# Loading a convolution filter by DMA in 64-byte runs, already in the layout of its first matmul, in place of transposing it on the matrix engine

## The chip, the cores and the metric

The kernel runs on one core of a Trainium2 chip. The metric is device time in microseconds (us), the median of several runs; lower is better. A ratio is computed as the mean time of one kernel's runs over that of the other's of the same rounds, so it is not quite the ratio of the medians quoted beside it.

## The reference, cut to what matters

The program is the forward and backward pass of two branches in parallel on a 2048 x 1024 bf16 input: a gated MLP (the larger part of the work) and a long convolution (H3) whose filter `ssm_k` is as long as the sequence. The convolution is written with FFTs:

```python
kv = k_shift * v                                  # (1, 2048, 1024)
kv_f = rfft2(pad(kv))                             # over time
kf_f = rfft2(pad(ssm_k))                          # ssm_k is (1024 channels, 2048 times)
y = irfft2(kv_f * kf_f)[:2048] + kv * ssm_D
out = x + xn * y + mlp(xn)                        # and the gradients of it all
```

One thing matters here: `ssm_k` lies in memory by channel, its times side by side, while `kv` and the gradients lie by time. The transform runs over time, so on the matrix engine time must lie on the partitions.

## The kernel before: the parts that the change and the argument touch

The convolution branch goes through 8 groups of 128 channels. Its transform is split in two steps of small matmuls with tables of sines. Its instructions are spread over slots between the MLP's matmuls, one slot per 8 of these, so that the matrix engine (PE) always has MLP work while ACT (ScalarE) and DVE (VectorE) serve the branch. The filter of a group is loaded with channels on the partitions, transposed on the matrix engine in sixteen pieces, and run through the first step:

```python
    def loads_1(self, gi):
        hn = self.ld.tile([P, 16, P], BF16, name="hn")
        self.load(hn[:].rearrange("p r c -> p (r c)"), self.ssm_k[cg, :])        # 128 rows of 4096 bytes
        ...                                                                      # gt, sD

    def h_tile(self, st):
        hT = self.ttile("hT")
        hv = st["hn"][:].rearrange("p r c -> p (r c)").rearrange("p (q r) -> p r q", r=16)
        pst = self.ps.tile([P, 16, P], BF16, name="pst", tag="aps")
        for r in range(16):
            self.pri.now()
            self.pri.pin(self.nc.tensor.transpose(pst[:, r, :], hv[:, r, :], self.identA[:]))
        self.act(hT[:, 0:16, :], pst[:])
        return hT

    def fwd1_filter(self, st, hT):                     # RH: the sine table R, with every other row zero
        B = st["Bh"] = self.big.tile([P, 64, NB1, 2], BF16, name="B", tag="big")
        for r0 in range(0, NB1, 8):                    # four steps, each in its own slot
            ps = self.ps.tile([P, 1024], F32, name="ps0", tag="aps")       # two PSUM buffers
            for jj in range(2):
                r = r0 % 16 + 4 * jj
                self.mm(ps[:, 512 * jj:512 * jj + 512], self.RH[:, r0 // 16]..., hT[:, r:r + 4, :]...)
            self.act(B[:, :, r0:r0 + 8, :], ps[:]...)                      # eviction on ACT
            yield
```

The gate gradient (`gt`, loaded by time) goes through the same first step in another form: 64 times on the lower and 64 on the upper half of the partitions, one matmul with 64 rows for each half.

```python
                for u in range(2):
                    rows = slice(64 * u, 64 * u + 64)
                    self.mm(ps[:, u]..., self.R[rows]..., src[rows, j:j + 4, :]...)
```

The names in the lines shown below: hn is the filter, gt the gate gradient, xt the normalised input by time, vt is v and kp is k; B is the result of a first step. The gate product is gt times xt, on DVE. wg, wu and wd are the gate, up and down weights of the MLP, and xnT its transposed input. An eviction is the copy of a result out of PSUM, the memory that the matmuls write to.

All loads of the branch, and nearly all others, are issued by the SyncE sequencer on one DMA queue (q1).

```python
    def steps(self):                                   # the start of the branch
        ...
        nx = self.loads_1(0); self.loads_2(nx)         # hn, gt, sD; kp, vt of group 0
        yield 10000 ... yield 13000 ... yield 9500     # waits, in ns of MLP work
        self.load_xn(nx)                               # xt of group 0
        hT = self.h_tile(nx)
        yield 2000
        ...                                            # the slots of group 0, 1, ... 7
```

## Time and profile before

| | before |
|---|---|
| median of the first 3 runs | 1920.11 us (1919.44 to 1923.64) |
| span of the profiled run | 1917.5 us |
| matrix engine (PE) busy | 98% |
| transposes / first-step matmuls of the filter | 128 / 64 |
| DMA packets, of them under 512 bytes | 628,002, 458,360 |

The lines that carry this are shown in the prediction. How to read them: a line of the timeline gives the start and the duration in us, then engine, source line, operation and tiles; `x8` is a run of eight instructions; brackets give the idle time before it and what ended it.

### The profile page before, as it was taken

The page shows a single profiled execution, that of the slowest core. Times are in us where ns is not written, and L with a number is a line of the kernel's source. Part 1 is how long each engine was busy: PE and PEld are TensorE (multiplying, and loading weights), DVE is VectorE, ACT ScalarE, POOL GpSimd, SP SyncE. Part 2 cuts the span into 40 slices and gives each one's busy share as a digit, 9 for nine tenths or more (in the row PEclk, how much of TensorE's full clock was granted, in tenths as well). Part 3 has the DMA queues.
Part 4 walks back from the last instruction along what each step waited for, and adds up shares of the span by engine and source line. Part 5 has one row for each costly group of instructions (what it writes and reads, how often), then busy time and mean ns, then how long its engine had stood idle before and what let it go on. Part 6 is the DMA issues. An engine that isn't in the chain of part 4 may idle for free.

```text
span 1917.5 us, 36080 instructions
## 1 busy us (share of the span) xinstructions
PE 1887.5 (98%) x15343; PEld 885.7 (46%) x15575; DVE 911.3 (48%) x1365; ACT 635.4 (33%) x868; POOL 15.8 (1%) x38
## 2 busy tenths in 40 slices
PE   8999999999999999999999999999999999999999
PEld 4444444444444444444444444444444544444444
DVE  6777767767767754544444354310212222222222
ACT  5854364364364354354344344321000000000000
POOL 1100000000000000000000000000000000000000
PEclk9999999999999999999999999999999999999999
DMA  9975878974975972655662633375999964444453
GB/s 248 290 178 136 184 184 184 222 184 133 186 182 136 251 218 78 176 132 179 153 170 90 170 100 122 100 206 208 266 240 239 241 156 121 121 121 121 121 121 72
DMA packets 628002, 323.16 MB, mean 169 GB/s; under 512 B 458360, under 2 KB 597376, under 8 KB 627840
## 3 DMA queue, kind: packets, MB, share of 16 engines
q1 hardware_dynamic: 617344, 299.99, 63.5%
q10 hardware_dynamic: 9216, 16.65, 2.8%
q0 software_dynamic: 1280, 4.20, 0.7%
q8 instruction: 122, 2.00, 0.4%
q14 instruction: 40, 0.33, 0.1%
HBM read 143.79 MB, written 95.44 MB: 125 GB/s over the span
## 4 chain that ended last, share of the span: by engine, by line
PE 95%; DMA 2%; issue 1%; DVE 1%; SPq 0%; ACT 0%; DVEq 0%; ACTq 0%
PE ps_x L1294 20%; PE ps_w L1067 19%; PE ps_h L818 10%; PE ps_o L1225 10%; PE ps_u L818 10%; PE ps_g L818 9%; PE ps_d L1067 8%; PE ps L72 7%; PE ps_d L1080 1%; DMA wu<-in_B_W_up_dram 1%; DMA ugs<-ug_d 0%; DMA ln_x<-in_A_q_dram 0%; PE pst L308 0%; PE ps_w L1080 0%; DMA xt<-xn_d 0%
## 5 line engine op out<-in xcount | busy, mean ns | idle before, releaser
L1067 PE MATMUL ps_w<-ugs,xn_nat 128*128 128x512 bf16 x1673 | 376.7, 379 | 5.3 <-issue 3.7
L818 PEld LDWEIGHTS <-xnT 128*128 128x128 bf16 x1792 | 170.1, 98 | 211.6 <-issue 10.3
L1067 PEld LDWEIGHTS <-xn_nat 128*128 128x128 bf16 x1728 | 165.0, 98 | 199.4 <-issue 5.5
L818 PE MATMUL ps_g<-wg,xnT 128*128 128x512 bf16 x862 | 202.5, 379 | 5.5 <-DVE xnT L853 1.9
L818 PE MATMUL ps_u<-wu,xnT 128*128 128x512 bf16 x868 | 204.5, 379 | 3.2 <-issue 1.4
L1312 ACT ACTIVATE w<-xn,m 128x512 f32<-128x512 bf16 x32 | 24.3, 807 | 553.0 <-issue 317.2
L818 PE MATMUL ps_h<-wdT,goT 128*128 128x512 bf16 x868 | 202.0, 379 | 2.6 <-issue 1.6
L1294 PE MATMUL ps_x<-wuT,guT 128*128 128x512 bf16 x878 | 197.5, 379 | 1.0
L1294 PE MATMUL ps_x<-wgT,ggT 128*128 128x512 bf16 x878 | 197.3, 379 | 0.9
L1225 PE MATMUL ps_o<-wd,hT 128*128 128x512 bf16 (+1 forms) x879 | 186.7, 372 | 0.9
L1067 PE MATMUL ps_d<-g_nat,hs 128*128 128x512 bf16 x740 | 167.7, 379 | 3.1 <-issue 2.4
L1294 PEld LDWEIGHTS <-guT 128*128 128x128 bf16 x896 | 87.7, 98 | 105.7
L1294 PEld LDWEIGHTS <-ggT 128*128 128x128 bf16 x896 | 87.7, 98 | 105.5
L1225 PEld LDWEIGHTS <-hT 128*128 128x128 bf16 x896 | 87.7, 98 | 100.0
L818 PEld LDWEIGHTS <-goT 128*128 128x128 bf16 x896 | 85.4, 98 | 102.9 <-issue 3.4
L319 DVE STREAM_TRANSPOSE flp<-C 128x1024 f32<-128x1024 f32 x48 | 90.5, 1931 | 81.7 <-ACT C L76 81.7
L921 DVE SCALAR_TENSOR_TENSOR ru<-ru,ps_u 128x512 bf16<-128x512 bf16 x112 | 76.6, 684 | 110.3 <-issue 48.9
L984 ACT CAST gh<-ps_h 128x512 bf16<-128x512 f32 x112 | 65.4, 585 | 159.0 <-PE ps_h L818 150.6
L76 ACT CAST C<-ps 128x1024 bf16<-128x1024 f32 x96 | 92.5, 1015 | 75.6 <-PE ps L72 74.6
L1171 ACT CAST wi<-ps_w 128x512 bf16<-128x512 f32 x108 | 63.7, 590 | 157.1 <-PE ps_w L1067 144.8
L319 DVE STREAM_TRANSPOSE flp<-B 128x1024 f32<-128x1024 f32 x48 | 90.5, 1935 | 50.4 <-ACT B L76 50.4
L1067 PEld LDWEIGHTS <-hs 128*128 128x128 bf16 x768 | 72.7, 98 | 88.9 <-issue 4.2
(176 smaller groups left out, 1479.7 us busy)
## 6 DMA issues: line engine op xcount, KB each, us to landing
ug_d<-ru SPq DMA_DIRECT2D x112, 256.0 KB
ugs<-ug_d SPq DMA_DIRECT2D x112, 256.0 KB
wg<-in_B_W_gate_dram SPq DMA_DIRECT2D x56, 256.0 KB
wu<-in_B_W_up_dram SPq DMA_DIRECT2D x56, 256.0 KB
h_d<-ht SPq DMA_DIRECT2D x112, 128.0 KB
hs<-h_d SPq DMA_DIRECT2D x56, 256.0 KB
out_dram<-wi SPq DMA_DIRECT2D x56, 256.0 KB
gt<-in_grad_out_dram SPq DMA_DIRECT2D x32, 256.0 KB
```

Source lines behind the costliest of these rows:

```text
L72: self.pri.pin(self.nc.tensor.matmul(out, lhsT=lhsT, rhs=rhs, start=start, stop=stop))
L76: self.pri.pin(self.nc.scalar.copy(out=out, in_=in_))
L319: self.pri.pin(self.nc.vector.transpose(out=df[:, c0:c0 + 32, :], in_=sf[:, c0:c0 + 32, :]))
L818: self.pri.pin(self.nc.tensor.matmul(ps[:], lhsT=xT[:, kt * P:(kt + 1) * P], rhs=w(kt), start=(kt == 0), stop=(kt == self.DT - 1)), always ...
L921: self.pri.pin(nc.vector.scalar_tensor_tensor(out=ru[s][:, 1, :], in0=ru[s][:, 0, :], scalar=0.0, in1=ps[:], op0=ALU.is_gt, op1=ALU.mult))
L984: self.pri.pin(nc.scalar.copy(out=gh[:], in_=ps[:]))
L1067: self.pri.pin(self.nc.tensor.matmul(ps[:], lhsT=lhsT(st), rhs=rhs(st), start=(st == 0), stop=(st == self.ST - 1)))
L1080: self.pri.pin(self.nc.tensor.matmul(ps[i][:], lhsT=lhsT(i, st), rhs=rhs(i, st), start=(st == 0), stop=(st == self.ST - 1)))
L1171: self.pri.pin(nc.scalar.copy(out=wo[0][:, d, :], in_=ps[:]))
L1225: nc.tensor.matmul(ps, lhsT=hT[:, kt, :], rhs=self.wd[:, kt, oc], start=(kt == 0), stop=(kt == self.FT - 1))
L1294: nc.tensor.matmul(ps, lhsT=T[:, kt, :], rhs=W[:, kt, oc], start=(i == 0), stop=(i == n - 1))
L1312: nc.scalar.activation(out=w[:, oc], in_=xn[:, oc], func=ACT.Identity, scale=m[:, 7:8], bias=m[:, 6:7])
```

## The change

Its intent: let the DMA do the transposing. It reads each channel's row in runs of 32 times (64 bytes) and writes every run to the partition of its time block. Sixteen transposes, an eviction and a half-empty table per group go; the first step becomes that of the gate gradient. The core of the diff (cut: declarations, passing of `hT`):

```diff
-        self.load(hn[:].rearrange("p r c -> p (r c)"), self.ssm_k[cg, :])
+        for ch in range(2):
+            c0 = gi * P + 64 * ch
+            self.load(hn[64 * ch:64 * ch + 64], self.ssm_k[c0:c0 + 64, :].rearrange("c (q n) -> q c n", n=NB1))
...
-    def h_tile(self, st):
-        ... (16 transposes and a copy)
...
+        for k0 in range(0, 4, 2):
+            for k in range(k0, k0 + 2):
+                ps = self.ps.tile([P, 2, 512], F32, name="ps0", tag="aps")
+                for ch in range(2):
+                    rows = slice(64 * ch, 64 * ch + 64)
+                    self.mm(ps[:, ch], self.R[rows]..., hn[rows, 16 * k:16 * k + 16, :]...)
+                self.act(B[:, :, 8 * k:8 * k + 8], ps[:]...)
             yield
...
-        hT = self.h_tile(nx)
-        yield 2000
...
         yield f1h, tk if gi == 0 else None
         yield f1h, tk
-        yield f1h, self.both(lambda: self.add_D(st), tk)
-        yield f1h, (lambda: self.gate_grad(st)) if gi == 0 else tk
+        yield None, self.both(lambda: self.add_D(st), tk)
+        yield None, (lambda: self.gate_grad(st)) if gi == 0 else tk
```

More of the change, by code (lines that the diff above doesn't have):

```diff
@@ L122, in tables @@
         self.R = con.tile([P, 2, 2, NB1], BF16, name="R")
-        self.RH = con.tile([P, 2, 2, 2, NB1], BF16, name="RH")
         self.RB = con.tile([P, 64], BF16, name="RB")
@@ L147, in tables @@
         n1 = pbit(63, 1.0, "n1p")
-        n1h = pbit(126, 0.5, "n1h")
-        up = pbit(1, 1.0, "up")
         def first(n, name):
@@ L160, in first @@
             return tr
-        tr = first(n1h, "H")
-        nup = lin(up, -1.0, 1.0, "nup")
-        for u, mu in ((0, nup), (1, up)):
-            V.tensor_scalar(out=self.RH[:, u], in0=tr[:], scalar1=mu[:], scalar2=None, op0=ALU.mult)
-        tr = first(n1, "R")
-        V.tensor_copy(out=self.R[:], in_=tr[:])
+        V.tensor_copy(out=self.R[:], in_=first(n1, "R")[:])
         e128 = con.tile([P, 1], F32, name="e128")
@@ L256, in loads_1 @@
         cg = slice(gi * P, (gi + 1) * P)
-        hn = self.ld.tile([P, 16, P], BF16, name="hn")
-        self.load(hn[:].rearrange("p r c -> p (r c)"), self.ssm_k[cg, :])
+        hn = self.ld.tile([P, 64, NB1], BF16, name="hn")
+        for ch in range(2):
+            c0 = gi * P + 64 * ch
+            self.load(hn[64 * ch:64 * ch + 64], self.ssm_k[c0:c0 + 64, :].rearrange("c (q n) -> q c n", n=NB1))
         gt = self.ld.tile([P, 16, P], BF16, name="gt")
@@ L299, in taps @@
                 yield
-    def h_tile(self, st):
-        hT = self.ttile("hT")
-        hv = st["hn"][:].rearrange("p r c -> p (r c)").rearrange("p (q r) -> p r q", r=16)
-        pst = self.ps.tile([P, 16, P], BF16, name="pst", tag="aps")
-        for r in range(16):
-            self.pri.now()
-            self.pri.pin(self.nc.tensor.transpose(pst[:, r, :], hv[:, r, :], self.identA[:]))
-        self.act(hT[:, 0:16, :], pst[:])
-        return hT
     def flip(self, st, key, src):
@@ L320, in flip, with fwd1_filter @@
             yield
-    def fwd1_filter(self, st, hT):
-        B = st["Bh"] = self.big.tile([P, 64, NB1, 2], BF16, name="B", tag="big")
-        for r0 in range(0, NB1, 8):
-            ps = self.ps.tile([P, 1024], F32, name="ps0", tag="aps")
-            for jj in range(2):
-                r = r0 % 16 + 4 * jj
-                self.mm(ps[:, 512 * jj:512 * jj + 512], self.RH[:, r0 // 16].rearrange("p e a l -> p (e a l)"),
-                        hT[:, r:r + 4, :].rearrange("p r c -> p (r c)"))
-            self.act(B[:, :, r0:r0 + 8, :], ps[:].rearrange("p (r cp i) -> p cp r i", r=8, i=2))
+    def fwd1_filter(self, st):
+        B = st["Bh"] = self.big.tile([P, 2, 32, NB1, 2], BF16, name="B", tag="big")
+        hn = st["hn"]
+        for k0 in range(0, 4, 2):
[3 more added lines that the diff above has]
+                    rows = slice(64 * ch, 64 * ch + 64)
+                    self.mm(ps[:, ch], self.R[rows].rearrange("p e a l -> p (e a l)"),
+                            hn[rows, 16 * k:16 * k + 16, :].rearrange("p c n -> p (c n)"))
+                self.act(B[:, :, 8 * k:8 * k + 8],
+                         ps[:].rearrange("p h (cp i n) -> p h cp n i", i=2, n=NB1))
             yield
@@ L334, in add_D @@
         for rows in (slice(0, 32), slice(64, 96)):
-            b0 = st["Bh"][rows, :, 0, :]
+            b0 = st["Bh"][rows].rearrange("p h cp n i -> p (h cp) n i")[:, :, 0, :]
             self.tt(b0, b0, st["sD"][rows].rearrange("p (cp i) -> p cp i", i=2), ALU.add)
@@ L490, in steps @@
         self.pri.strict = True
-        hT = self.h_tile(nx)
-        yield 2000
         for gi in range(self.NG):
             st, nx = nx, None
-            for p, d in self.slots(st, hT, gi):
+            for p, d in self.slots(st, gi):
                 self.run(p)
@@ L498, in steps, with slots @@
                 yield self.SLOT
-            nx, hT = st.get("nx"), st.get("hT_next")
+            nx = st.get("nx")
         self.small_outputs()
-    def slots(self, st, hT, gi):
+    def slots(self, st, gi):
         last = gi + 1 == self.NG
@@ L518, in next_gate @@
                 self.gate_grad(st["nx"])
-        def next_h():
-            if not last:
-                st["hT_next"] = self.h_tile(st["nx"])
         def start_kvt():
@@ L541, in slots @@
         tk = self.taps(st, ksh, kp, [(3, 0), (2, 1), (1, 2), (0, 3)])
-        f1h = self.fwd1_filter(st, hT)
+        f1h = self.fwd1_filter(st)
         f1g = self.fwd1(st, "Bg", gt)
@@ L545, in slots @@
         yield f1h, tk
-        yield f1h, self.both(lambda: self.add_D(st), tk)
-        yield f1h, (lambda: self.gate_grad(st)) if gi == 0 else tk
+        yield None, self.both(lambda: self.add_D(st), tk)
+        yield None, (lambda: self.gate_grad(st)) if gi == 0 else tk
         yield None, tk
-        flH = self.flip(st, "fH", st["Bh"][:])
+        flH = self.flip(st, "fH", st["Bh"][:].rearrange("p h cp n i -> p (h cp) n i"))
         yield f1g, flH
@@ L630, in slots @@
         yield None, tg
-        yield next_h, None
+        yield None, None
         self.store_time(self.out_gk, st["cg"], gk)
```

## The prediction

> **What bounds the kernel now.** I read the page first: the busy shares, the strip of slices, the chain that ended last.
>
> ```profile
> PE 1887.5 (98%) x15343; PEld 885.7 (46%) x15575; DVE 911.3 (48%) x1365; ACT 635.4 (33%) x868; POOL 15.8 (1%) x38
> ...
> PEclk9999999999999999999999999999999999999999
> DMA  9975878974975972655662633375999964444453
> ...
> PE 95%; DMA 2%; issue 1%; DVE 1%; SPq 0%; ACT 0%; DVEq 0%; ACTq 0%
> ```
>
> The matrix engine is busy in every slice, at the full clock, and 95% of the chain is on it. Nothing else is near its limit over the whole span, so PE time removed is time removed, one for one, and work for ACT or DVE matters only if PE has to wait for it. Where it waits now, the list of waits of PE says:
>
> ```profile
> PE ps_w L1067 <- issue: 3.7, 23, 0.2
> ...
> PE ps_u L818 <- DMA wu<-in_B_W_up_dram: 0.5, 2, 0.3
> ...
> PE ps_g L818 <- DMA wg<-in_B_W_gate_dram: 0.4, 1, 0.4
> PE ps L72 <- ACT hT L76: 0.2, 1, 0.2
> ```
>
> (total us, times, longest us). All waits of PE sum to under 20 us. The three small ones at the end matter here: one on the hT copy that the change removes, and three on weight loads, all between 95 and 110 us. The strip shows DMA at 9 in the first two slices (0 to 96 us). So the start is a stage of its own, where transfers have no slack. The same stretch by tens of microseconds:
>
> ```profile
> core 0: us, PE busy (x) PEld busy (x) DVE busy (x) ACT busy (x) POOL busy (x), PEclk, DMA share, GB/s
> ...
> 70.00:80.00 10.00, 9.95 (x47) 4.58 (x47) 9.64 (x37) 9.57 (x16) 0.00 (x0) 1.00 1.24 213
> 80.00:90.00 10.00, 9.95 (x47) 4.52 (x47) 6.18 (x20) 9.95 (x18) 1.09 (x2) 1.00 1.21 269
> 90.00:100.00 10.00, 9.72 (x56) 4.97 (x56) 5.58 (x10) 7.20 (x11) 1.07 (x2) 1.00 0.94 294
> 100.00:110.00 10.00, 9.39 (x44) 3.92 (x44) 6.78 (x10) 4.30 (x6) 0.00 (x0) 1.00 1.16 242
> 110.00:120.00 10.00, 9.79 (x109) 4.32 (x111) 9.93 (x10) 7.20 (x10) 0.00 (x0) 1.00 0.53 140
> ```
>
> The DMA share (last but one) is over 1 where packets overlap, and stays near 1 until 110 us, when it falls.
>
> **What the change touches on PE**, from the timeline (start us, duration us, group). The transposes of one group of 128 channels:
>
> ```profile
> 93.08 0.81 PE L818 MATMUL ps_u<-wu,xnT 128*128 128x512 bf16 x3
> 93.72 1.18 PE L308 MATMUL pst<-ident,hn 128*128 128x128 bf16 x16
> 94.74 0.38 PE L818 MATMUL ps_u<-wu,xnT 128*128 128x512 bf16 x1
> ```
>
> The duration includes the pipeline's tail; from start to next start PE is taken 94.74 - 93.72 = 1.02 us. The filter's first step before, and the gate gradient's first step, which already has the form that the filter's gets:
>
> ```profile
> 251.38 0.59 PE L72 MATMUL ps<-hT,RH 128*128 128x512 bf16 x2
> 251.81 1.89 PE L818 MATMUL ps_u<-wu,xnT 128*128 128x512 bf16 x8
> 253.54 1.89 PE L818 MATMUL ps_h<-wdT,goT 128*128 128x512 bf16 x8
> 255.36 0.60 PE L72 MATMUL ps<-gt,R 64*128 64x512 bf16 x4
> 255.90 1.90 PE L818 MATMUL ps_h<-wdT,goT 128*128 128x512 bf16 x7
> ```
>
> Two 128-row matmuls take 0.43 us (0.216 each). Four 64-row ones take 0.54 us, plus 0.09 before them: eight matmuls from 253.54 at 0.216 end at 255.27, the next starts at 255.36. So four cost 0.63 us, less than the 0.86 that four full ones would.
>
> **What the Trainium skill says.** "TensorE: Matmul & The Clock Gate", section "Back-to-back issue gap": N/2.4 + 2.5 ns, 216 ns at N = 512; the trace agrees (1.73 us for eight). The same page, "Part 3: Packing small matmuls — row/col tiling": matmuls on different row groups run at the same time; the trace agrees, less the 0.2 us of gaps at the switch. "DMA: Bandwidth & Descriptors", section "Why small descriptors are slow (HBM only)": every packet has a fixed part. The trace's packet records agree: median 46 ns for 1024 bytes, 18 for 256, 9 for 4. The same page, "Queues, rings and completion order": each engine consumes one queue's descriptors in ring order, so what is issued behind a long transfer on that queue starts later. Nearly all loads here are on one queue (q1, 63.5% of the engines' time).
>
> **The change part by part.**
>
> PE, per group: minus 1.02 (sixteen transposes), minus 4 x 0.43 = 1.72 (eight full matmuls in four steps), plus 2 x 0.63 = 1.26 (eight half-height ones in two steps): minus 1.48 us. Over eight groups minus 11.8 us. The 64-row halves replace 128-row matmuls in whose table half of the entries were zero; the matmul count stays 64 in all, so the gain there is from pairs running side by side.
>
> ACT: minus eight copies of hT (1.87 us each), same number of B evictions (about 1.0 us). It is 33% busy, so this is worth nothing by itself. But two evictions now follow each other in each of two *consecutive* slots (the gate gradient's are two slots apart), with two PSUM buffers. After the step at 259.46 the two evictions ended at 261.99, 2.53 us later; the next slot's second pair comes about 1.73 + 0.63 + 0.22 = 2.58 us after the first start. With a cast of 0.59 us ahead of them on ACT it can be 0.2 us late. I add 0.2 us a group, 1.5 us in all.
>
> DVE and tables: one table (RH), its sine and its scalings go, at a time when they hide. Nothing.
>
> DMA: hn per group was 128 packets of 4096 bytes, about 160 to 180 ns each, so 128 x 170 / 16 = 1.4 us of all engines. It becomes 128 x 64 = 8192 packets of 64 bytes, 65,536 over the kernel on top of 628,002. How long one takes no row shows. Between the 4-byte and 256-byte medians, 11 ns would be the line; but the strided 256-byte loads of gt, kp, vt and xt from HBM move only about 640 packets a microsecond (25 ns a packet on each engine, against 18 for the other 256-byte ones), and no microsecond of the trace that I looked at moved more than about 1100 packets. I choose 22 ns: 8192 x 22 / 16 = 11.3 us a group, 10 us more than before (6 at the floor of 1100 a microsecond, 15 at 33 ns).
>
> In seven of the groups this should hide: the load is issued some 70 slots before its use, and 26 us before the next weight load (hn issued at 116.2, 259.8, 403.4 and 547.7; gate weights at 142.2, 285.8, 429.6, 573.7). In between the packet records show idle stretches of about 10 us (132 to 139, 273 to 283, 419 to 426, 563 to 570). Later the slabs are read a whole slab ahead.
>
> Not so in the first. hn is issued at 72.7 us, wg at 93.95, wu at 98.76, and PE already waits for wu:
>
> ```profile
> 106.31 0.38 PE L818 MATMUL ps_u<-wu,xnT 128*128 128x512 bf16 x1 [0.16 <-DMA wu<-in_B_W_up_dram]
> 107.03 3.02 PE L818 MATMUL ps_u<-wu,xnT 128*128 128x512 bf16 x12 [0.34 <-DMA wu<-in_B_W_up_dram]
> ```
>
> Of the 10 us more, about 2.7 can be absorbed in the queue's idle time from 89.5 to 92.2 and 1 in the thinner traffic of 92 to 98. The rest, 6.3 us, moves wu back, and PE with it. The 1.5 us that PE saves in this group before 107 us are lost in the same wait, since the load ends it.
>
> Sum: minus 11.8 + 1.5 (first group's gain lost) + 6.3 (later weights) + 1.5 (evictions) = minus 2.5 us; 1920.1 becomes about 1917.5. I put it at 1917.
>
> **The rivals.**
>
> *The load hides everywhere.* For it: the use of hn itself is 20 us after its issue even at the start, and if 64-byte packets come near 11 ns the delay is under 3 us. Against it: PE's waits on wg and wu show no slack at all. It would make 1908 to 1910.
>
> *The load chokes the queue in every group.* At 50 ns a packet, one load holds the queue for 26 us. The stores of h and of the gradients behind it then come late, their six-deep buffers don't come free, ACT and DVE can't empty PSUM, and PE stops some 5 to 10 us in each group, besides 20 us at the start: 1950 to 1985. Against it: no packet under 512 bytes in this trace has a median near that; the 256-byte ones at their worst are 33 to 36. For it: thousands of 64-byte reads, 4096 bytes apart, are a pattern that this kernel doesn't have yet.
>
> *The pairs don't overlap or PSUM becomes the wait.* If each half-height matmul cost a full one, PE would save only the 8.2 us of transposes, and the sum would be plus 2. The gate gradient's identical form speaks against it.
>
> **Range and chances.** The PE side is sure to 2 us. The packet cost is the spread: 11 to 16 ns gives 1908 to 1912, 22 gives 1917, 33 gives 1923, and dearer ones a tail. So 1908 to 1928. Faster by over 2% (below 1882) would need three times more than everything PE saves: 0.01. Slower by over 2% (above 1958) needs the choked queue: 0.06.
>
> **What would show it.** Right: no group for pst, 64 matmuls from hn and R in pairs, PE's time between two MLP groups around them near 0.63 us; the DMA packet count up by some 64,500; the wait of PE on wu (or wg) near 105 to 115 us grown to several microseconds, and no such wait in later groups. Wrong: PE waits behind hn, or behind ru and ht stores, at each group's start (packets dearer than thought); or no larger wait at the start and a time near 1909 (cheaper, or absorbed); or PE waits of over 0.5 us on the B evictions in each group.

## The result, and the profile after

The changed kernel takes 1915.13 us (median of 4, 1913.07 to 1918.11) against 1920.76 before (median of 4): ratio 0.9973, interval 0.9959 to 0.9987. Faster by a quarter of a per cent, the same by the measure of 2%. The page of the changed kernel, busy times, packets and chain:

```profile
PE 1898.4 (99%) x15447; PEld 872.8 (46%) x15447; DVE 908.9 (48%) x1355; ACT 617.7 (32%) x858; POOL 15.0 (1%) x37
...
DMA packets 692640, 323.13 MB, mean 169 GB/s; under 512 B 524024, under 2 KB 663040, under 8 KB 692480
...
PE 97%; DMA 1%; DVE 1%; ACT 0%; SPq 0%; issue 0%; DVEq 0%; ACTq 0%
```

The span is 1912.6 us. PE's busy sum is *larger* than before although it has less to do: the profile of before lacks 232 matmul records (15343 matmuls against 15575 weight loads), this one lacks none. So the busy sums of the two can't be subtracted. Starts can. The filter's first step in the second group, timeline of PE:

```profile
245.29 1.89 PE L799 MATMUL ps_h<-wdT,goT 128*128 128x512 bf16 x8
247.11 0.60 PE L72 MATMUL ps<-hn,R 64*128 64x512 bf16 x4
247.65 1.90 PE L799 MATMUL ps_h<-wdT,goT 128*128 128x512 bf16 x8
```

Eight matmuls from 245.29 at 0.216 us end at 247.02; the four of the filter start 0.09 later and take 0.54: 0.63 us, as worked out from the gate gradient.

Where PE still waits (total us, times, longest):

```profile
PE ps_g L799 <- DVE xnT L834: 3.5, 2, 3.2
PE ps L72 <- DVE gt L80: 2.1, 1, 2.1
...
PE ps L72 <- ACT B L76: 0.9, 2, 0.5
```

The first line is from the layer norm at 34 us, which the change doesn't touch. The third is the evictions, in one group of eight. The second is the first group. The timeline of PE there, and of DVE:

```profile
104.04 3.62 PE L799 MATMUL ps_g<-wg,xnT 128*128 128x512 bf16 x16
109.80 0.61 PE L72 MATMUL ps<-gt,R 64*128 64x512 bf16 x4 [2.14 <-DVE gt L80]
110.33 5.31 PE L799 MATMUL ps_u<-wu,xnT 128*128 128x512 bf16 x16
```

```profile
108.51 1.23 DVE L80 TENSOR_TENSOR gt<-gt,xt 128x2048 bf16<-128x2048 bf16 x1 [2.39 <-DMA xt<-xn_d]
```

PE stands for 2.14 us because the gate product waits for xt, which stands in the queue behind the filter. The load alone does not explain this wait: counted from a fixed point of the MLP's work (weight load 192 of the ruler below), the product starts at 62.9 us here and at 63.4 in the kernel before, but PE is ready for it at 62.1 here, and at 68.2 there. In the two later profiles of the change the product itself is late, at 68.9 (r1) and 66.1 us (r3). Then sixteen matmuls take 5.31 us instead of 3.62: the window from 110 to 120 us shows why (before it was at 1.00; third value from the right):

```profile
110.00:120.00 10.00, 10.00 (x81) 3.80 (x78) 8.65 (x10) 4.66 (x6) 0.00 (x0) 0.83 0.76 136
```

The clock of PE was halved for 3.41 us (the trace's clock record: 110.39 to 113.80), which costs 1.7 us more. The load itself, from SyncE's timeline, in the first and the second group:

```profile
73.77 4.45 SPq L88 DMA_DIRECT2D hn<-in_A_ssm_k_dram x2
78.26 3.34 SPq L88 DMA_DIRECT2D gt<-in_grad_out_dram x2
...
115.61 3.24 SPq L88 DMA_DIRECT2D hn<-in_A_ssm_k_dram x2
```

SyncE issues two DMAs of 4096 packets each. In the packet records the 64-byte packets of the first group run from 75.6 to 81.6 us, some 6 us; in the second, from 117.0 to 122.1, some 5. Their median is 11 ns each.

**A ruler for the rest.** The start of the kernel scatters from run to run (the layer norm waits for its first loads), so spans of single profiles can't be compared to a microsecond. Every weight load of PE is in the trace, though, so I counted those of all but the convolution branch, in order, and took the times of number 192 (about 42 us, after the scatter of the start), number 640 (about 146 us, in the first group) and number 8192 (near the end). Between them lies the same MLP work in every kernel, and beside it the same slots of the branch.

```
kernel (profile)               192 to 640   640 to 8192
before                             104.6        1766.5
before, second profile             105.0        1765.6
changed                            105.6        1756.8
changed, second profile            111.5        1758.6
changed, third profile             107.1        1757.6
```

In the seven later groups the changed kernel gains 7 to 10 us (8.4 between the means). In the first it should gain 1.5 and loses 1 to 7 instead.

### The profile page after: what moved, and what is told of

It reads as the page before. It is cut to its first block, busy times and chain, and to the rows that moved or that the text cites. A ratio compares the mean times of both kernels' runs of the same rounds, so it can differ in the third digit from the quotient of the medians.

```text
span 1912.6 us, 36039 instructions
## 1 busy us (share of the span) xinstructions
PE 1898.4 (99%) x15447; PEld 872.8 (46%) x15447; DVE 908.9 (48%) x1355; ACT 617.7 (32%) x858; POOL 15.0 (1%) x37
## 4 chain that ended last, share of the span: by engine, by line
PE 97%; DMA 1%; DVE 1%; ACT 0%; SPq 0%; issue 0%; DVEq 0%; ACTq 0%
PE ps_x L1275 20%; PE ps_w L1048 20%; PE ps_u L799 10%; PE ps_h L799 10%; PE ps_o L1206 10%; PE ps_g L799 10%; PE ps_d L1048 9%; PE ps L72 6%; PE ps_d L1061 1%; PE ps_w L1061 1%; DMA ln_x<-in_A_q_dram 1%; DMA xt<-xn_d 0%; PE ps_r L1236 0%; DMA wu<-in_B_W_up_dram 0%; PE pst_x L831 0%; ACT ln_j L727 0%
## 5 line engine op out<-in xcount | busy, mean ns | idle before, releaser
L1048 PE MATMUL ps_w<-ugs,xn_nat 128*128 128x512 bf16 x1728 | 382.9, 379 | 0.0
L799 PE MATMUL ps_g<-wg,xnT 128*128 128x512 bf16 x896 | 207.0, 382 | 3.9 <-DVE xnT L834 3.5
L1275 PEld LDWEIGHTS <-guT 128*128 128x128 bf16 x896 | 87.7, 98 | 105.7
L1277 DVE CUSTOM_DVE_ANT_0 gx<-ps_x,gy 128x512 f32<-128x512 f32 x32 | 22.1, 691 | 182.1 <-PE ps_x L1275 182.1
```

The lines of the kernel that those rows point to most:

```text
L799: self.pri.pin(self.nc.tensor.matmul(ps[:], lhsT=xT[:, kt * P:(kt + 1) * P], rhs=w(kt), start=(kt == 0), stop=(kt == self.DT - 1)), always ...
L1048: self.pri.pin(self.nc.tensor.matmul(ps[:], lhsT=lhsT(st), rhs=rhs(st), start=(st == 0), stop=(st == self.ST - 1)))
L1275: nc.tensor.matmul(ps, lhsT=T[:, kt, :], rhs=W[:, kt, oc], start=(i == 0), stop=(i == n - 1))
```

## The experiments

Theory A: the 64-byte load of the first group holds the queue, where transfers have no slack; all later ones hide. Theory B: the loss at the start comes from the dropped step of 2000 ns, which moves the gate product nearer to xt's load. Rival C: the missing part is spread over all groups.

**r1, the changed kernel again, and r2, the kernel before again.**

> The changed kernel once more, to see what repeats. Fixed: about 5.5 us under the kernel before (ratio near 0.997). Open: in the first profile of the changed kernel 3.3 us more than before were lost by 40 us into the span, in code that the change does not touch (PE waited 3.2 us for an xnT copy, and its clock was then halved for 3.4 us). If that is chance (a load landing late at the start), this profile need not have it, and the span is then 2 to 4 us shorter. If it belongs to the change, it is there again. The wait at the first group (2.1 us, PE on the gate product gt) should be there in both cases.

> The kernel before once more, against itself: ratio 1.000 within 0.002. Its profile shows whether the late load at the start (30 to 40 us) also falls on this kernel at times. If the start is chance, it may show a wait of 1.5 to 3.5 us there; waits at 105 to 107 us should stay under 1.5 us in total.

r1: 1913.22 us (1911.97 to 1918.35), ratio 0.9962. r2: 1918.95, ratio 0.9993 (0.9980 to 1.0005), as it should be. The late start does not belong to the change: r1's profile has 1.1 us in place of 3.2 for that wait, and no other profile has more than 1.8 at that place. But r1's span was not shorter. With an earlier start PE ran into the queue harder. Timeline of PE, r1:

```profile
97.67 0.39 PE L72 MATMUL ps<-hn,R 64*128 64x512 bf16 x2 [1.59 <-ACT B L76]
...
103.29 1.32 PE L799 MATMUL ps_g<-wg,xnT 128*128 128x512 bf16 x4 [0.76 <-DMA wg<-in_B_W_gate_dram]
...
106.48 2.32 PE L799 MATMUL ps_g<-wg,xnT 128*128 128x512 bf16 x10 [0.81 <-DMA wg<-in_B_W_gate_dram]
...
111.45 0.88 PE L72 MATMUL ps<-gt,R 64*128 64x512 bf16 x4 [2.65 <-DVE gt L80]
```

Waits on an eviction, on wg three times, on gt, then the halved clock: the stretch took 111.5 us. The profiled run was the slowest of r1's five (1918.35); the others took 1912 to 1915.4, so a loss of 7 us is not the usual one.

**e1, the first filter not loaded** (zeros instead; wrong result), **and e2, the step put back.**

```diff
+        if gi == 0:
+            self.nc.gpsimd.memset(hn[:], 0.0)
-        for ch in range(2):
+        for ch in range(2 if gi else 0):
```

> The changed kernel with the first group's filter set to zero by GpSimd and not loaded (wrong result for that group on purpose); the other seven loads stay. Theory A (the 8192 small packets of the first load hold the queue at the start, everything behind them comes some 6 us late): the wait of PE at about 107 us on gt or wu goes to under 0.7 us, its clock is not halved there, and the kernel is 3 to 4 us faster than the changed one. Theory B (what is lost there comes from the dropped step of 2000 ns ahead of the first slot, which brings the gate product nearer to the load of xt): the wait on gt stays near 2 us and the time is the changed kernel's within 1 us.

```diff
         self.pri.strict = True
+        yield 2000
         for gi in range(self.NG):
```

> The changed kernel with the dropped step of 2000 ns ahead of the first slot put back, nothing else. Theory A: PE waits as long in total around 107 us, on wu if not on gt, and the time is that of the changed kernel within 1 us. Theory B: the wait on gt falls under 0.5 us, no clock halving, 3 to 4 us faster than the changed kernel.

e1: 1912.63 us, ratio 0.9959; against r1's 1913.22 it is 0.6 us faster, not 3 to 4. e2: 1911.54, ratio 0.9956, 1.7 us faster than r1 by the medians; the intervals of the three overlap. By the times neither expectation was met. The profiles say more. Waits of PE in e1, and timeline of PE in e2:

```profile
PE ps L72 <- DVE gt L80: 1.6, 1, 1.6
```

```profile
103.88 1.53 PE L800 MATMUL ps_g<-wg,xnT 128*128 128x512 bf16 x4 [2.71 <-DMA wg<-in_B_W_gate_dram]
106.67 1.01 PE L800 MATMUL ps_g<-wg,xnT 128*128 128x512 bf16 x2 [1.27 <-DMA wg<-in_B_W_gate_dram]
```

In e1 the wait on gt is still there, without the load: so theory B is right about *this* wait, in part. In e2 it is gone, and in the profiled run PE waits 4.2 us for wg instead, with the clock halved for 6.8 us. But that run is the slowest of e2's five (1915.08). Three of the others had the full clock throughout (a granted clock of 1.000) and took 1911.0 to 1911.5, so this profile is not e2's usual run and does not rule theory B out. The stretch from 192 to 640 took 103.4 us in e1 and 111.4 in e2. e1's is near what before's 104.6 becomes with the group's 1.5 us off; the first profile of the change, which started nearly as late as e1, took 105.6.

The time of e1 can't be compared as it stands, because the edit most likely had a cost of its own: weight load 192 came 4.4 us later than before. Timelines of GpSimd (POOL) and of DVE in e1, then of DVE in r3:

```profile
9.26 1.82 POOL L251 MEMSET hn<- 128x2048 bf16 x1
```

```profile
8.56 4.45 DVE L758 TENSOR_SCALAR ln_x<-ln_x,ln_s 128x1024 bf16<-128x1024 bf16 x1
```

```profile
8.50 0.49 DVE L756 TENSOR_SCALAR ln_x<-ln_x,ln_s 128x1024 bf16<-128x1024 bf16 x1
```

GpSimd writes the zeros at the very start of the kernel, and the DVE instruction of the layer norm that runs beside it takes 4.45 us; in the 13 other profiles it takes 0.49. PE then waits 3.2 us, and its clock is halved for 6.8. That the zeros are the cause rests on this one profile; but all five runs of e1 have a granted clock of 0.998 or 0.999, as such a start would give. With 4.4 us taken off, e1 would be near 1908 us (an estimate from this profile), 5 under r1, on the side of theory A. As built, its time decides nothing; e7 tests theory A better.

**e3 and e4, the whole branch 35 us later, in both kernels.**

```diff
-A_START = 45_000
+A_START = 80_000
```

> The kernel before with the whole convolution branch started 35 us of matrix time later (start value 80 instead of 45), so that its first loads go out after the weights of the second block instead of ahead of them. Control for e4: the waits at 105 to 107 us (0.5 to 1 us) go, so 0 to 1.5 us faster than before; if the shifted loads or the later end of the branch collide with something else, it shows here as well.

> The changed kernel with the same later start. Theory A (the matrix work saved is 1.48 us in each of eight groups, and what is missing in the total is lost in the first group's collision at the start of the kernel): against e3 it is 11 us faster (11.8 less some 0.9 for waits on the evictions), and its time is near 1908. Rival C (what is missing is spread over all groups: evictions, queue, or a saving per group that is smaller than worked out): it stays 5 to 7 us under e3.

e3: 1933.67 us, ratio 1.0062. e4: 1925.12, ratio 1.0020. Both slower. Waits of PE, first in e3, then in e4:

```profile
PE ps_u L818 <- DMA wu<-in_B_W_up_dram: 4.5, 2, 3.8
PE ps_o L1225 <- DMA wd<-in_B_W_down_dram: 4.4, 1, 4.4
```

```profile
PE ps_o L1206 <- DMA wd<-in_B_W_down_dram: 5.2, 2, 4.8
PE ps_u L799 <- DMA wu<-in_B_W_up_dram: 3.5, 2, 2.8
PE ps_g L799 <- DMA wg<-in_B_W_gate_dram: 2.4, 2, 2.2
```

The branch's transfers now collide with weight loads of other blocks, and its later end delays the load of wd. e4 is 8 us under e3 (1.0020 / 1.0062 = 0.9958), between the 11 of theory A and the 5 to 7 of C, and e4 has waits on wg (2.4 us) that e3 hardly has (0.2). This pair decides nothing. It suggests that the schedule sits in a narrow gap between transfers.

**e5, full-height matmuls on a padded table.**

```diff
-                    self.mm(ps[:, ch], self.R[rows]..., hn[rows, 16 * k:16 * k + 16, :]...)
+                    self.mm(ps[:, ch], self.RZ[:, ch]..., hn[:, 16 * k:16 * k + 16, :]...)   # RZ: R, other half zero
```

> The changed kernel, but each pair of 64-row matmuls becomes two 128-row ones on a table padded with zeros (same load, no transposes, same number of matmuls, right result). If the pairs of the change run side by side as the timeline of the gate gradient says, a step of four goes from 0.63 to 0.86 us of PE, so 2 x 8 x 0.23 = 3.7 us are given back: ratio to the changed kernel 1.0019. If the 64-row pairs gave nothing, no difference.

Timeline of PE, second group:

```profile
243.13 1.03 PE L72 MATMUL ps<-hn,RZ 128*128 128x512 bf16 x4
244.00 1.89 PE L802 MATMUL ps_h<-wdT,goT 128*128 128x512 bf16 x8
```

0.87 us for a step of four, against 0.63. So the pairs of the change do run side by side, and are worth 2 x 0.24 = 0.5 us a group. From 640 to 8192 the profile takes 1759.5 us, 0.9 to 2.7 more than the three profiles of the change, where 3.1 were due (7 x 2 x 0.24, less 0.3 of waits on evictions that it doesn't have): the same sign, and too coarse for the size. The time, 1915.56 us and ratio 0.9971 (0.9957 to 0.9986), doesn't separate it from the change (0.9957 to 0.9973): 3 us are near the scatter.

**e6, twice the packets in the later groups.**

```diff
+            for h in range(0, NB1, 16 if gi else NB1):
+                e = h + (16 if gi else NB1)
+                self.load(hn[64 * ch:64 * ch + 64, :, h:e], src[:, :, h:e])
```

> The changed kernel with the filter of groups 2 to 8 loaded in 32-byte runs: twice the packets (16384 a group), the same bytes; the first group's load is as in the change. The packets took 11 ns of an engine at 64 bytes, and the load held the queue some 6 us; twice that, about 12 us, is what the prediction had assumed. If the load hides in these groups with room to spare, the time is the changed kernel's within 1 us and PE shows no new wait after 125 us. If the queue is at its limit, waits on wg, wu or on buffers appear in each group and it is 3 us or more slower.

1914.29 us, ratio 0.9967. The 32-byte packets have a median of 9 ns, and a group's load now fills the queue from 117.0 to 127.4 us, 10.4 us. After 125 us PE waits for the evictions in one group (0.9 us, as in the change) and 0.2 us once for wu. From 640 to 8192: 1757.3 us, the change's. So the load hides in the seven later groups even at twice its length, and the rival of a choked queue is out, with room to spare.

**r3, e7, e8 and e9: take something else out of the crowded queue.** e7 loads the first group's v behind the second block's weights; e8 does the same in the kernel before; e9 adds the step of e2 and puts a slot between the two filter steps. The diff of e7, cut:

```diff
-        vt = ...; self.load_time(vt, self.v, cg)         # in loads_2
+        if st["gi"]: self.load_v(st)
...
-        yield None, tk
+        yield (lambda: self.load_v(st)) if gi == 0 else None, tk
         flH = self.flip(
```

> The changed kernel a third time, as the anchor of this call: ratio to the kernel before 0.996 to 0.9975.

> The changed kernel, the first group's v (2048 packets of 256 bytes, 3.2 us of the queue at the 640 a microsecond seen in the trace of before) loaded after the second block's weights instead of ahead of them. That takes back two thirds of the 4.6 us by which the 64-byte load is longer than the old one. Theory A (the queue ahead of wg and wu sets when PE goes on at about 107 us): PE resumes 3 us earlier there, waits of PE at 95 to 115 us fall from 2 to 7 us to under 3 us, and the time is 2 to 4 us below the anchor. If the loss does not hang on what is queued there: anchor within 1 us.

> Control: the kernel before with the same later load of v. It waits under 1 us there, so it can win at most 1 us (ratio 0.9995 to 1.0).

> The changed kernel with the later v of e7, the step of 2000 ns put back (e2), and the two filter steps one slot apart, so that their evictions have two slots (waits on ACT B, 0.3 to 3 us in the profiles so far, should go). If the three are what was missing: 3 to 5 us below the anchor, near 1909, and no wait of PE over 1 us after 60 us.

| | median us | ratio to before | 95% | 192 to 640 |
|---|---|---|---|---|
| r3, the change | 1912.95 | 0.9957 | 0.9944 to 0.9969 | 107.1 |
| e7, v later | 1910.65 | 0.9945 | 0.9930 to 0.9959 | 103.5 |
| e8, before with v later | 1919.25 | 0.9990 | 0.9977 to 1.0002 | 104.4 |
| e9, combined | 1910.66 | 0.9947 | 0.9935 to 0.9960 | 105.7 |

Timeline of PE in e7:

```profile
104.53 0.61 PE L72 MATMUL ps<-gt,R 64*128 64x512 bf16 x4 [0.90 <-DVE gt L80]
...
106.47 0.59 PE L803 MATMUL ps_u<-wu,xnT 128*128 128x512 bf16 x2 [0.37 <-DMA wu<-in_B_W_up_dram]
```

With 2048 packets of 256 bytes out of the way the waits of PE at the start fall to 1.4 us in all, none halves the clock, and the stretch takes 103.5 us: before's less the group's saving, near enough. From 640 to 8192, though, e7's profile takes 1.5 us more than r3's, with no wait that explains it; over both stretches it is 2.0 us ahead. The time is 2.3 us under the anchor, as theory A had it: the two intervals overlap, but four of e7's five runs are faster than the fastest of r3. In the kernel before, which had no such loss, the same edit gives 0.9990, where that kernel against itself gave 0.9993 (r2). So what is queued ahead of wg and wu sets most of the loss in the first group. Rival C is left with about 1 us: the seven later groups gained 8.4 of the 9.5 us (7 x 1.48, less 0.9 for evictions) that theory A has there. e9 fell short of its expectation (2.3 us under the anchor in place of 3 to 5): the waits on gt and on evictions are gone, as meant, but PE waits for weights instead, probably because the step puts their loads at another moment (two of these four waits are in later groups):

```profile
PE ps_u L804 <- DMA wu<-in_B_W_up_dram: 2.8, 4, 1.3
```

Once v is out of the way, the step of e2 thus gains nothing more. e7, the simpler, is the version to keep: 0.55% under the kernel before; the 0.1% under the change is within the overlap of the intervals.

## Why the prediction was right or wrong

The time was right: 1917 predicted with a range of 1908 to 1928, 1915.13 measured (1913 later). "Within 2%" had 0.93 (1 - 0.01 - 0.06). That it came so near is in part luck. With the packet at its measured 11 ns the prediction's own sum gives 1911.8 (the load 4.2 us longer than before, 0.5 of it not absorbed: -11.8 + 1.5 + 0.5 + 1.5 = -8.3), below what was measured; the packet that was too dear stood in for waits and a halved clock that the prediction did not have. Step by step:

- **PE, minus 1.48 us a group: right.** The step takes 0.63 us as worked out. Over the seven later groups the gain is 1.0 to 1.4 us a group between single profiles and 1.20 between the means, or 1.33 with the 0.9 us of eviction waits put back; about 1 us of the seven groups' 10.4 is not accounted for. e5 shows the part that comes from the pairs. (The 216 ns of a matmul follow the formula that the prediction cites from "Back-to-back issue gap"; that section gives the formula for an isolated matmul, and about 131 ns for a stream of them in a real kernel, which this trace contradicts: eight in 1.73 us.)
- **Evictions, plus 1.5 us: right in kind, and too large.** 0.9 us, all in one of the later groups; in two profiles 2.1 (r1) and 2.4 us (e6) more in the first group.
- **ACT, DVE and tables, nothing: no run spoke against it.**
- **A 64-byte packet, 22 ns: wrong, and the largest mis-sized term.** It measured 11 ns, the line between the 4- and the 256-byte medians, which I had named and turned down for the slower rate of the strided 256-byte loads. The load held the queue for some 6 us, not 11.3; against the 1.4 of the old one 4.6 more, not 10.
- **Hidden in seven groups: right.** Waits on a weight load in later groups are at most 0.5 us (0.4 and 0.5 in r1, 0.2 in r3, none in the first profile; before has one of 0.35), and 0.2 us in all at twice the packets (e6).
- **First group, plus 6.3 us and the group's own 1.5 lost: right in mechanism, its two halves wrong in opposite directions.** Half the packet time would have left some 2 us by my sum (4.6 less the 3.7 absorbed, and PE 1.5 earlier). The profiles show losses against before of 1.0, 2.5 and 6.9 us. What I missed is the halved clock after a wait: 1.7 us for each 3.4 us of it, in the first group of two of the three profiles of the change. The step that failed is "the rest moves wu back, and PE with it": PE mostly stood earlier, on wg and on the gate product behind xt. Part of the wait on the gate product comes from the dropped step of 2000 ns (e1, e2), which I had not looked at: PE is ready for the product 6 us earlier than before, of which the saving explains 1.5.
- **Readings and sums of the prediction that don't hold:** of the three waits on weights "between 95 and 110 us" the one on wg (0.35 us) is at 487 us; the "idle stretches of about 10 us" are 7 to 10 us long; and without overlap of the pairs its sum would be plus 1 and not plus 2 (-8.2 + 1.5 + 6.3 + 1.5 = 1.1). None of these decides the result.
- **What is still open:** the usual loss in unprofiled runs. By the ratios it is 11.8 - 0.9 less 5 to 8 us, so 3 to 6 us of the first group; the profiled runs, a few each, scatter too much to say which waits make it up. The granted clock gives a part: it was 1.000 in 29 of 32 runs of the kernel before, and in 3 of 14 of the change, 0.998 or 0.999 in the others. One halving of 3.41 us takes off 0.0009, so the change had about one a run, wherever in the run it fell: some 1.4 us more than before (an estimate).

## What to carry to other kernels

Work that the busiest engine does on data in the wrong layout can go to the DMA even in 64-byte runs, if the load is issued long before its use: the time of the queue it takes was hidden here in seven cases of eight. Before doing so, find the one place where the queue has no slack (mostly the start), count what stands ahead of the next load that the engine will need, and move something else out of it. What a short wait costs there may be more than its length: 2.14 us of it cost 1.7 us more here. And look at what an experiment adds as well as at what it removes: the zeros of e1 most likely cost 4 us of their own.

## What the Trainium skill lacked or had wrong

- "TensorE: Matmul & The Clock Gate", Part 1 and "Why this matters for your kernels": it says that the clock goes back to half after an idle window of about 3.4 us, and to allow no gaps over about 3 us. Here much less was enough. In the clock records of all 14 profiles every change of the clock lies on a grid of 3.41 us. Counted by the cells of this grid (without the start-up and the end of the kernel), the clock was halved after each of the 11 cells in which PE stood for 1.83 us or more in all, and after none of the others, of which the idlest had 1.82 (r3). So neither 3 us nor the length of a single wait is the measure on this kernel: 2.14 us (the change, at 107.7) and 1.88 us with 0.52 soon after (e6, 2.15 within the cell) halved it; 2.18 us that the grid cut in two (e4, at 239; at most 1.55 in a cell) did not.
- "DMA: Bandwidth & Descriptors", section "Why small descriptors are slow (HBM only)": it gives the mechanism, but no time of a small packet on its engine (the page's one figure per packet, about 10.5 ns, is the whole time of a 4 KB transfer divided by its packets). Measured medians: 4 bytes 9 ns, 32 bytes 9 ns, 64 bytes 11 ns, 256 bytes 18 ns, 1024 bytes 46 ns. A load of 8192 packets of 64 bytes moved at some 1400 to 1600 packets a microsecond, while SyncE took 3.2 to 4.5 us to issue its two DMAs. I found no page with the pace at which one queue is fed many short runs.
- "TensorE: Matmul & The Clock Gate", Part 4, gives about 275 ns for a PE transpose in a kernel. That is a duration; here each lasted 219 to 235 ns, but sixteen in a row held PE for 1.02 us, 64 ns each, and that is what removing one is worth.
